# Moving left-over squares and late sums one place down ScalarE's list in the opening steps of a fused convolution and SoLU kernel

## The chip, the cores and the metric

The program runs on one core of a Trainium2 chip. The metric is the device time of one execution in microseconds (us), taken as the median of several runs. Each engine of the core (TensorE = PE, VectorE = DVE, ScalarE = ACT, GpSimd = POOL, SyncE = SP, which issues the transfers) works through a list of its own in order; semaphores tie the lists together.

## The reference

`x` is 8 x 4160 x 192. A causal convolution with 7 taps per head (softmax of `weight`) gives 33280 tokens of 192, and a SoLU layer follows:

```python
out = np.einsum('hk,bskhg->bshg', w, x_unf)        # convolution, 7 taps, 8 heads
h = x @ w_in                                       # 192 -> 1024
e = np.exp(h - h_max)
sm = e / (np.sum(e, axis=-1, keepdims=True) + 1e-09)
solu = h * sm
mu = np.mean(solu, axis=-1, keepdims=True)
var = np.mean((solu - mu) ** 2, axis=-1, keepdims=True)
ln = (solu - mu) / np.sqrt(var + 1e-06) * g_ln
return (ln @ w_out).astype(np.float32)             # 1024 -> 192
```

## The kernel before

The 33280 tokens are 260 tiles of 128 tokens. `x` is also cut into chunks: chunk 0 has 1024 rows (tiles 0 to 7), chunks 1 and 2 feed tiles 8 to 15 and 16 to 24 or so, and so on. A chunk is loaded, its size is measured (`sum_squares`: ACT squares or DVE maxima, "sums of x"), a scale is worked out by a short run of DVE instructions (`scale_steps`), and its convolution is done on PE in pieces (`product`, tiles `pc`). The result leaves PSUM as two fp16 parts: the upper by ACT (`upper`, line 313), the lower by DVE (`lower`, line 322), both into `y16`, which a transfer transposes into `yT`. From chunk 3 on the convolution takes `x` in two fp16 halves: `halve_steps` makes them in three steps for each piece of five windows: the upper half `xs` (ACT for chunk 3, line 234), the scaling of `x` (POOL, line 240) and the lower half (POOL, line 243). These steps lie in a `Queue` with a cost for each; `queue.run(budget)` puts as many of them into the lists as the budget allows.

A tile goes through these instructions: eight matmuls and a few small ones into `ph` (lines 736 and 759), `emit_max` (DVE, line 790), `emit_exp` (ACT, line 797), `emit_mul` (DVE, line 807), `emit_hi` (ACT cast to the fp16 half `p16`, line 815), `emit_lo` (POOL, the other half, line 827, and the transposing transfer `pT`, line 829), `emit_square` (ACT, line 819, a sum of squares for the variance), and some five tiles later `emit_out` (PE, `po`, line 859) and `emit_evac` (DVE, lines 867 and 869). `po`, `pc` and `tph` (a matmul that spreads the taps) take turns in two PSUM banks (`single`), so each of them waits until the one before the last has been read. `tph` is copied out by two small ACT casts (line 583).

From tile 8 on three tiles a, b, c form one call of `three_steps(i)`, for i = 8, 11, 14, 17, 20 and so on. The program is written by hand in the order of the lists: what is called earlier stands earlier on its engine. Calls with i < 16 (8, 11 and 14) have `start` set. What a call leaves over (the square of its last tile, in some calls also of tile b) is kept in `squares` and done in the next call by `root_squares()`. `late` holds sums of x that were put off. The last square of a group of eight tiles also puts the group's `steps` (POOL's inverse root) into the queue.

Of the kernel before, what the change touches and what calls it, by code (L numbers as in the profile page):

```python
# [19 lines left out]
def kernel(  # L20
# [533 lines left out]
    for e, bank in enumerate(banks):  # L554
        for q in range(2 * per):
# [4 lines left out]
                start=q == 0, stop=q == 2 * per - 1,  # L560
# [233 lines left out]
    def emit_exp(t):  # L794
        g, grp = t.g, t.grp
        t.e = sp.tile([P, F], F32, name=f"e_{t.i}", tag="e", bufs=4)
        act.activation(  # L797
            t.e, t.ph, AF.Exp, bias=t.bias, scale=-1.0, accum_out=grp.z[:, g : g + 1]
        )
# [12 lines left out]
    def emit_hi(t):  # L812
        t.halves = t.e.rearrange("p (n f) -> p n f", n=NH)
        t.p16 = sp.tile([P, NH, 2, 512], F16, name=f"p16_{t.i}", tag="p16", bufs=4)
        act.copy(t.p16[:, :, 0, :], t.halves)  # L815

    def emit_square(t):
        junk = sp.tile([P, F], F32, name=f"sq_{t.i}", tag="sq", bufs=1)
        act.activation(  # L819
            junk, t.e, AF.Square, accum_out=t.grp.s2[:, t.g : t.g + 1]  # L820
        )
        if t.g == t.grp.n - 1 and t.g:
            t.grp.squares()
            queue.put(t.grp.steps(), first=True)

    def emit_lo(t, eng):
        eng.tensor_tensor(t.p16[:, :, 1, :], t.halves, t.p16[:, :, 0, :], ALU.subtract)  # L827
        t.pT = sp.tile([P, 2 * NFC, P], F16, name=f"pT_{t.i}", tag="pT", bufs=4)
        nc.sync.dma_start_transpose(t.pT, t.p16.rearrange("p n a f -> p (n a f)"))
# [231 lines left out]
    queue, groups, chain, rooted, rows, stores = Queue(), {}, [], [], [], []  # L1061

    def follow(c, i):

        chain.extend(
            (c.add_up, i + 1 + (c.ch > 1)) if f is None else (f, None)
            for f in c.scale_steps()
        )

        def go():  # L1070
            c.scaled = True
            if c.exact:
                return
            for j in range(c.np):
                queue.put(c.halve_steps(j, quick=c.ch == 3), (c.ch, j))

        chain.append((go, None))
# [8 lines left out]
    def take_rooted():  # L1086
        for g, age in rooted:
            if age:
                g.ready = True
                rows.extend(g.waiting)  # L1090
        rooted[:] = [(g, 1) for g, age in rooted if not age]
# [25 lines left out]
    PAIRED = FIRST // P  # L1117
    assert spans[0][2] == PAIRED * P and PAIRED == 8 and (NT - PAIRED) % 3 == 0
    early, doubles, squares, late, moves = [], [], [], [], []
# [12 lines left out]
    def sum_up(c, h, i):  # L1132
        c.sum_squares(*h)
        if c.sums == 2 * c.np:
            c.square_peaks()
            follow(c, i)
# [158 lines left out]
    def three_steps(i):  # L1295
# [19 lines left out]

        start = i < 2 * PAIRED

        soon = i in (FIRST // P * 2 + 1, FIRST // P * 3 + 2)
        if not start:
            loads(work)  # L1320
# [16 lines left out]
        def second():  # L1337
            for d in done[1:2]:
                emit_out(d)
            place(2)  # L1340
# [4 lines left out]
        def uppers(n):  # L1345
            for k, pc, hg in at(n):
                if not k.scaled and k.exact:
                    run_chain(20)
                k.upper(pc, *hg)

        def lowers(n):
            for k, pc, hg in at(n):
                k.lower(pc, *hg)

        def move():

            for f in moves[:1]:
                f()
            del moves[:1]

        def root_squares():
            for q in squares:
                emit_square(q)
            squares.clear()

        def opens():
            for k in work.get("open", []):
                k.open(lefts[k.ch], chunks[k.ch - 1])

        def turns():  # L1370
            moves.extend(
                lambda k=k, q=q: k.turn(*q) for k, q in work.get("turn", [])
            )

        def openings():
            opens()
            turns()
            while moves:
                move()
# [13 lines left out]
        if start:  # L1393
            emit_max(a)
            emit_exp(a)
            if i == PAIRED:
                for k, h in late:
                    sum_up(k, h, i - 1)
        if not start:
            root_squares()  # L1400
        add(0)
        if not start:
# [6 lines left out]
        emit_max(b)  # L1409
        lowers(1)  # L1410
        emit_exp(b)
        if start:
            root_squares()
            second()
            if i > PAIRED:
                for k, h in late:
                    sum_up(k, h, i - 1)
                late.clear()
                uppers(2)
            for k, q in doubles:  # L1420
                k.double(*q)
            doubles.clear()
# [3 lines left out]
            late[:] = after  # L1426
        emit_hi(a)
        emit_lo(a, pool)
        move()
        if urgent:  # L1430
            openings()
# [55 lines left out]
            chunks[5].load(0)  # L1487
        emit_lo(c, pool)
        squares.append(c)
        if urgent:  # L1490
            for k, q in work["double"]:
                k.double(*q)
        elif start:
            openings()
            doubles.extend(work.get("double", []))
        else:
            opens()
            if not soon:
                turns()
            move()  # L1500
            doubles.extend(work.get("double", []))
        if i == NT - 6:
            ready(b)
        queue.run(3.8 if i < 20 else 2.0)
        take_rooted()

    def ready(t):
        emit_z(t)
        emit_root(t)
# [58 lines left out]
    for i in range(PAIRED, NT - 3, 3):  # L1568
        three_steps(i)
# [28 lines left out]
```

## Time and profile before

| what | value |
|---|---|
| runs | 1162.34, 1166.07, 1166.71 us (median 1166.07) |
| profiled execution, first to last instruction | 1161.5 us; its own whole time is not listed beside it |
| PE busy | 1132.2 us, 97% of the span |
| DVE, ACT, POOL busy | 1016.8, 998.0, 878.6 us |
| mean granted PE clock | 0.999 |

The span is 0.84 us under the fastest run and 4.6 us under the median. In the profile's rows a time is from the span's start; "idle before, releaser" is how long the engine stood still before the instruction and which instruction ended most of that.

### The profile page before, as it was taken

Reading aid. Unit: us, or ns where it says so; the run is one execution under the profiler, and the core shown is the slowest. Engines: PE = TensorE matmul, PEld = TensorE weight load, DVE = VectorE, ACT = ScalarE, POOL = GpSimd, SP = SyncE. Lnnn points to the kernel's source line nnn. Section 1 sums busy time; section 2 is a strip of 40 time slices with the busy share of each in tenths; the row PEclk is TensorE's granted clock in tenths of the full one; section 3 lists DMA queues with packets and bytes.
Section 4 is the critical chain, followed back from the end, with each engine's and each line's share of the span. In section 5 each row is a group of like instructions: output and inputs, shape, how many; then the busy total and the mean of one; then the engine's idle time right before and its main releaser. Section 6 shows DMA issues by size and latency. Waiting matters only on the chain.

```text
span 1161.5 us, 22374 instructions
## 1 busy us (share of the span) xinstructions
PE 1132.2 (97%) x7742; PEld 692.4 (60%) x7742; DVE 1016.8 (88%) x2058; ACT 998.0 (86%) x1775; POOL 878.6 (76%) x686
## 2 busy tenths in 40 slices
PE   5898999999999999999999999999999999999998
PEld 3575566656666665655656666665666566566556
DVE  8888898988989898998889989888898988788787
ACT  6998988888888888888888888898888889888886
POOL 2745879987888588887868888588788858855665
PEclk9999999999999999999999999999999999999999
DMA  8799899999999999999999999999999998999988
GB/s 226 171 181 180 185 218 205 205 201 202 200 213 195 195 186 220 207 189 199 202 198 190 208 209 199 187 202 208 206 204 198 195 193 170 174 177 186 181 163 188
DMA packets 727391, 226.95 MB, mean 195 GB/s; under 512 B 651614, under 2 KB 725870, under 8 KB 727278
## 3 DMA queue, kind: packets, MB, share of 16 engines
q1 hardware_dynamic: 727278, 225.53, 100.2%
q8 instruction: 60, 0.98, 0.3%
q14 instruction: 53, 0.43, 0.1%
HBM read 33.00 MB, written 25.56 MB: 50 GB/s over the span
## 4 chain that ended last, share of the span: by engine, by line
PE 88%; DVE 5%; ACT 2%; DMA 2%; issue 2%; POOL 1%; SPq 0%; DVEq 0%; ACTq 0%; POOLq 0%
PE po L859 40%; PE ph L736 36%; PE pc L281 6%; PE ph L759 5%; DVE e L807 1%; DMA pT<-p 1%; DVE ph L790 1%; DMA raw_in<-in_moe_w_in_dram 1%; ACT e L797 1%; ACT sq L819 0%; DVE raw L869 0%; DVE y L322 0%; POOL p L827 0%; PE mean L701 0%; DVE wlo L647 0%
## 5 line engine op out<-in xcount | busy, mean ns | idle before, releaser
L827 POOL TENSOR_TENSOR p<-e,p 128x1024 f16<-128x1024 f32 x257 | 548.3, 2138 | 219.5 <-ACT p L815 218.0
L859 PE MATMUL po<-ohl,pT 128*128 128x192 f16 (+1 forms) x4264 | 539.8, 283 | 7.8 <-DVE raw L869 5.4
L859 PEld LDWEIGHTS <-pT 128*128 128x128 f16 x4264 | 384.4, 98 | 167.1 <-issue 7.6
L736 PE MATMUL ph<-whi,yT 128*128 128x512 f16 x1548 | 419.1, 380 | 2.7 <-DVE e L807 2.6
L790 DVE TENSOR_SCALAR_CACHE_REDUCE ph<-ph,cv 128x1024 f32<-128x1024 f32 x248 | 319.1, 1288 | 72.9 <-PE ph L759 56.6
L797 ACT ACTIVATE e<-ph,sm 128x1024 f32<-128x1024 f32 x260 | 289.4, 1113 | 102.0 <-DVE ph L790 95.8
L807 DVE SCALAR_TENSOR_TENSOR e<-ph,cv,e 128x1024 f32<-128x1024 f32 x248 | 317.1, 1279 | 26.0 <-ACT e L797 25.7
L736 PEld LDWEIGHTS <-yT 128*128 128x128 f16 x2064 | 192.6, 98 | 231.3 <-issue 36.3
L815 ACT CAST p<-e 128x1024 f16<-128x1024 f32 x257 | 266.8, 1039 | 27.9 <-DVE e L807 27.3
L819 ACT ACTIVATE sq<-e 128x1024 f32<-128x1024 f32 x260 | 273.4, 1052 | 0.2
L736 PE MATMUL ph<-wlo,yT 128*128 128x512 f16 x516 | 153.5, 379 | 0.0
L869 DVE TENSOR_REDUCE raw<-po 128x192 f32<-128x384 f32 x247 | 136.3, 552 | 14.3 <-PE po L859 13.9
L243 POOL TENSOR_TENSOR xs<-xr,xs 128x960 f16<-128x960 f32 (+1 forms) x56 | 107.6, 1922 | 1.4
L313 ACT ACTIVATE y<-pc 112x432 f16<-112x432 f32 (+5 forms) x140 | 62.8, 469 | 13.8 <-PE pc L281 8.1
L759 PE MATMUL ph<-wlo,yT 64*128 64x512 f16 x269 | 74.0, 380 | 0.0
L322 DVE SCALAR_TENSOR_TENSOR y<-pc,y 112x432 f16<-112x432 f32 (+5 forms) x140 | 72.2, 532 | 0.8 <-ACT y L313 0.8
L281 PE MATMUL pc<-xs,taps_hi 128*112 128x240 f16 (+1 forms) x448 | 72.9, 261 | 0.0
L759 PE MATMUL ph<-wlo,y 64*128 64x512 f16 x251 | 68.6, 380 | 0.0
L181 DVE TENSOR_REDUCE xa<-xr 128x1 f32<-128x384 f32 x112 | 66.6, 617 | 0.0
L281 PEld LDWEIGHTS <-taps_hi 128*112 128x112 f16 x448 | 52.4, 130 | 16.4
L240 POOL TENSOR_SCALAR xr<-xr,s 128x960 f32<-128x960 f32 (+1 forms) x56 | 57.5, 1027 | 2.9
L281 PE MATMUL pc<-xs,taps_lo 128*112 128x240 f16 (+1 forms) x224 | 58.5, 261 | 0.0
(148 smaller groups left out, 787.6 us busy)
## 6 DMA issues: line engine op xcount, KB each, us to landing
out_dram<-raw SPq DMA_DIRECT2D x127, 192.0 KB, 3.0
xr<-in_x_dram SPq DMA_DIRECT2D x41, 480.0 KB, 4.7
xr<-in_x_dram SPq DMA_DIRECT2D x22, 384.0 KB, 4.1
pT<-p SPq DMA_TRANSPOSE x263, 4.6
y<-yT SPq DMA_DIRECT2D x15, 140.0 KB, 3.1
y<-yT SPq DMA_DIRECT2D x15, 126.0 KB, 3.1
yT<-y SPq DMA_TRANSPOSE x102, 3.7
raw_out<-in_moe_w_out_dram SPq DMA_DIRECT2D x1, 1536.0 KB
```

The source lines that it names most:

```text
L243: (2.1 * size + 0.2, lambda: pool.tensor_tensor(xl, r, h, ALU.subtract)),
L281: nc.tensor.matmul(o, tp[:, h + j, :], r, start=q == 0, stop=q == len(ops) - 1)
L736: nc.tensor.matmul(bank, lhs, w[:, r, n * 512 : (n + 1) * 512], start=start and j == 0, stop=stop and j == len(ops) - 1,)
L759: nc.tensor.matmul(banks_of(t)[n], y[q, t.off : t.off + P], wlo[q, 1, n * 512 : (n + 1) * 512], start=start, stop=not start,)
L790: dve.tensor_scalar(t.ph, t.ph, t.cv[:, 0:1], None, ALU.mult, ALU.min, accum_out=t.bias)
L797: act.activation(t.e, t.ph, AF.Exp, bias=t.bias, scale=-1.0, accum_out=grp.z[:, g : g + 1])
L807: dve.scalar_tensor_tensor(t.e, t.ph, t.cv[:, 3:4], t.e, ALU.mult, ALU.mult, accum_out=t.grp.s1[:, t.g : t.g + 1],)
L815: act.copy(t.p16[:, :, 0, :], t.halves)
L819: act.activation(junk, t.e, AF.Square, accum_out=t.grp.s2[:, t.g : t.g + 1])
L827: eng.tensor_tensor(t.p16[:, :, 1, :], t.halves, t.p16[:, :, 0, :], ALU.subtract)
L859: nc.tensor.matmul(t.po[:, 0:n], t.pT[:, a, :], w, start=j == 0, stop=j == len(ops) - 1)
L869: dve.tensor_reduce(t.grp.raw[:, t.g, :], t.po[:, 0 : 2 * D].rearrange("p (a d) -> p d a", a=2), AX.X, ALU.add,)
```

## The change

Four edits. In the calls with `start` (8, 11, 14) `root_squares()` and, for 11 and 14, the late sums go from right after the second exponential to behind the first cast (`emit_hi(a)`) and `emit_lo(a)`. In call 17 (`behind`) `root_squares()` goes from ahead of the first maximum to behind the second exponential. At the end of call 14 (`held`) the last `queue.run` is left out, so what it put into the lists comes with the next one, in the middle of call 17.

```diff
+        behind = i == 2 * PAIRED + 1
...
-        if not start:
+        if not start and not behind:
             root_squares()
...
         emit_exp(b)
+        if behind:
+            root_squares()
         if start:
-            root_squares()
             second()
             if i > PAIRED:
-                for k, h in late:
-                    sum_up(k, h, i - 1)
-                late.clear()
                 uppers(2)
...
         emit_hi(a)
         emit_lo(a, pool)
+        if start:
+            root_squares()
+            if i > PAIRED:
+                for k, h in late:
+                    sum_up(k, h, i - 1)
+                late.clear()
         move()
...
         squares.append(c)
+        held = i + 3 == 2 * PAIRED + 1
...
-        queue.run(3.8 if i < 20 else 2.0)
+        if not held:
+            queue.run(3.8 if i < 20 else 2.0)
```

The lists of PE, DVE and SP keep their order; those of ACT and POOL change. In the rows below the number behind a tile's name is that of the tile or chunk (`e_12` is tile 12, `xs_3` is chunk 3), the last number is only a counter.

ACT in call 8, before, from the second exponential on:

```order
L797 ACTIVATE e_9_761,z_8_690<-ph_9_729,sm_9_759 128x1024
L819 ACTIVATE sq_7_763,s2_0_270<-e_7_646 128x1024
L917 ACTIVATE t1_0_271<-z_0_268,cv_0_168 128x8
L921 ACTIVATE t2_0_272<-s1_0_269 128x8
L313 ACTIVATE y16_2_0_809<-pc_2_0_0_792,s_2_754 112x5x96
L815 CAST p16_8_811<-e_8_748 128x2x512
L819 ACTIVATE sq_8_825,s2_8_692<-e_8_748 128x1024
L815 CAST p16_9_828<-e_9_761 128x2x512
L313 ACTIVATE y16_2_0_809<-pc_2_0_4_841,s_2_754 112x5x32
```

and after:

```order
L797 ACTIVATE e_9_761,z_8_690<-ph_9_729,sm_9_759 128x1024
L313 ACTIVATE y16_2_0_805<-pc_2_0_0_788,s_2_754 112x5x96
L815 CAST p16_8_807<-e_8_748 128x2x512
L819 ACTIVATE sq_7_812,s2_0_270<-e_7_646 128x1024
L917 ACTIVATE t1_0_271<-z_0_268,cv_0_168 128x8
L921 ACTIVATE t2_0_272<-s1_0_269 128x8
L819 ACTIVATE sq_8_825,s2_8_692<-e_8_748 128x1024
L815 CAST p16_9_828<-e_9_761 128x2x512
L313 ACTIVATE y16_2_0_805<-pc_2_0_4_841,s_2_754 112x5x32
```

The square of tile 7 and its group's two small rows now stand behind the copy of the convolution and the cast of tile 8, so that copy is the next thing after the exponential. In calls 11 and 14 the same happens: in 11 two squares (tiles 9 and 10) and two sums of x change places with one copy (line 313) and the cast of tile 11; in 14 the squares of tiles 12 and 13 with two copies and the cast of tile 14.

POOL from the end of call 14 to call 20, before:

```order
L827 TENSOR_TENSOR p16_16_1232<-e_16_1215,p16_16_1232 128x2x512
L243 TENSOR_TENSOR xs_3_1227<-xr_3_0_329,xs_3_1227 128x960
L240 TENSOR_SCALAR xr_3_1_333<-xr_3_1_333,s_3_1054 128x960
L827 TENSOR_TENSOR p16_17_1311<-e_17_1304,p16_17_1311 128x2x512
L243 TENSOR_TENSOR xs_3_1227<-xr_3_1_333,xs_3_1227 128x960
L240 TENSOR_SCALAR xr_3_2_557<-xr_3_2_557,s_3_1054 128x960
L243 TENSOR_TENSOR xs_3_1227<-xr_3_2_557,xs_3_1227 128x960
L827 TENSOR_TENSOR p16_18_1348<-e_18_1308,p16_18_1348 128x2x512
```

and after:

```order
L827 TENSOR_TENSOR p16_16_1232<-e_16_1215,p16_16_1232 128x2x512
L827 TENSOR_TENSOR p16_17_1308<-e_17_1299,p16_17_1308 128x2x512
L243 TENSOR_TENSOR xs_3_1227<-xr_3_0_329,xs_3_1227 128x960
L240 TENSOR_SCALAR xr_3_1_333<-xr_3_1_333,s_3_1054 128x960
L827 TENSOR_TENSOR p16_18_1344<-e_18_1303,p16_18_1344 128x2x512
L243 TENSOR_TENSOR xs_3_1227<-xr_3_1_333,xs_3_1227 128x960
L240 TENSOR_SCALAR xr_3_2_557<-xr_3_2_557,s_3_1054 128x960
L243 TENSOR_TENSOR xs_3_1227<-xr_3_2_557,xs_3_1227 128x960
```

Each piece of chunk 3's lower half comes one `p16` later on POOL: the half of piece 1 (the row that reads `xr_3_1` into `xs_3`) now has the `p16` of tiles 17 and 18 ahead of it, where it had only that of tile 17. PE's first convolution of chunk 3, in call 20, reads pieces 0 and 1.

ACT in call 17, before, from the cast of tile 16 to that of tile 17:

```order
L815 CAST p16_16_1232<-e_16_1215 128x2x512
L234 ACTIVATE xs_3_1227<-xr_3_0_329,s_3_1054 128x960
L234 ACTIVATE xs_3_1227<-xr_3_1_333,s_3_1054 128x960
L583 CAST taps_hi_135<-tph_2_1276 128x2x8x14
L583 CAST taps_lo_136<-tph_2_1276 128x2x8x14
L936 ACTIVATE raw_0_550<-raw_0_550,t2_0_272 128x192
L819 ACTIVATE sq_16_1299,s2_16_1062<-e_16_1215 128x1024
L797 ACTIVATE e_17_1304,z_16_1060<-ph_17_1267,sm_17_1302 128x1024
L797 ACTIVATE e_18_1308,z_16_1060<-ph_18_1281,sm_18_1306 128x1024
L815 CAST p16_17_1311<-e_17_1304 128x2x512
```

and after:

```order
L815 CAST p16_16_1232<-e_16_1215 128x2x512
L234 ACTIVATE xs_3_1227<-xr_3_0_329,s_3_1054 128x960
L583 CAST taps_hi_135<-tph_2_1273 128x2x8x14
L583 CAST taps_lo_136<-tph_2_1273 128x2x8x14
L936 ACTIVATE raw_0_550<-raw_0_550,t2_0_272 128x192
L797 ACTIVATE e_17_1299,z_16_1060<-ph_17_1264,sm_17_1297 128x1024
L797 ACTIVATE e_18_1303,z_16_1060<-ph_18_1278,sm_18_1301 128x1024
L819 ACTIVATE sq_16_1305,s2_16_1062<-e_16_1215 128x1024
L815 CAST p16_17_1308<-e_17_1299 128x2x512
```

The upper half of piece 1 has gone behind the cast of tile 17 and the square of tile 16 behind both exponentials, so the two exponentials of call 17 have two long rows fewer ahead of them, and the cast of tile 17 one.

## The prediction

> **What bounds the kernel now.** First the page's share of each engine and the chain, then busy time by stretches, then PE's waits inside the stretch that the change touches.
>
> ```profile
> PE 1132.2 (97%) x7742; PEld 692.4 (60%) x7742; DVE 1016.8 (88%) x2058; ACT 998.0 (86%) x1775; POOL 878.6 (76%) x686
> ...
> PE 88%; DVE 5%; ACT 2%; DMA 2%; issue 2%; POOL 1%; SPq 0%; DVEq 0%; ACTq 0%; POOLq 0%
> ```
>
> ```profile
> 80.00:126.50 46.50, 41.11 (x284) 25.42 (x283) 36.25 (x78) 40.60 (x76) 28.77 (x25) 1.00 0.94 183
> 126.50:137.00 10.50, 10.30 (x74) 6.44 (x72) 10.28 (x21) 10.06 (x19) 10.42 (x6) 1.00 0.75 154
> 137.00:1155.00 1018.00, 1015.69 (x6937) 616.77 (x6937) 899.25 (x1806) 878.58 (x1554) 799.74 (x616) 1.00 1.03 197
> ```
>
> The columns are PE, its weight loads, DVE, ACT, POOL, the granted clock, DMA. From 137 us on PE stands still for 2.3 of 1018 us: whatever PE has lost or won by then arrives at the end almost one for one. Before, in the calls that are changed (8 to 17, about 65 to 126 us), PE is idle for 5.4 us, by this view of its waits from 80 to 140 us:
>
> ```profile
> PE po L859 <- DVE raw L869: 5.0, 5, 1.8
> PE pc L281 <- DVE y L322: 0.5, 1, 0.5
> PE tph L577 <- DVE y L322: 0.2, 1, 0.2
> ```
>
> So the prize is 5.7 us at most, 0.28 of it after the change's last place. PE waits for DVE to empty a PSUM bank, and DVE is late because it waits for ACT. ACT is 40.6 of 46.5 us busy; a new order moves its work, it takes none away.
>
> **The change, call by call.** Each number is a shift of the same row of before.
>
> *Call 8.* Rows of the timelines of DVE, ACT and PE:
>
> ```profile
> 71.53 0.15 DVE L112 TENSOR_SCALAR s<-s 128x1 int32<-128x1 int32 x1
> 70.67 1.05 ACT L819 ACTIVATE sq<-e 128x1024 f32<-128x1024 f32 x1
> 72.09 0.64 ACT L313 ACTIVATE y<-pc,s 112x480 f16<-112x480 f32 x1
> 75.67 0.81 ACT L313 ACTIVATE y<-pc,s 112x160 f16<-112x160 f32 x2
> 76.51 0.84 DVE L322 SCALAR_TENSOR_TENSOR y<-pc,s,y 112x160 f16<-112x160 f32 x2 [0.56 <-ACT y L313]
> 77.50 1.04 PE L281 MATMUL pc<-xr,taps 128*112 128x120 f32 x8
> ```
>
> The copy at 72.09 needs the scale `s`, ready at 71.68. Before, the square fills that time. Now the copy is next at 70.67 and ACT stands still until about 71.72: it wins 0.37 us for the copy and loses 1.05 for all that comes after the square. The copy at 75.67 starts 1.05 later, DVE's part at 76.51 with it (it was waiting for ACT by 0.56 already), and PE's convolution at 77.50 is released by it: it started 0.15 after DVE's end at 77.35. PE loses 1.05. Exponential, DVE product and cast follow each other from here without a gap in which 1.05 could be made up, and all carry it into call 11.
>
> *Call 11.*
>
> ```profile
> 83.96 1.05 ACT L819 ACTIVATE sq<-e 128x1024 f32<-128x1024 f32 x1
> 83.87 1.04 PE L281 MATMUL pc<-xr,taps 128*112 128x120 f32 x8
> 87.64 0.64 ACT L313 ACTIVATE y<-pc,s 112x480 f16<-112x480 f32 x1
> 88.32 0.72 DVE L322 SCALAR_TENSOR_TENSOR y<-pc,s,y 112x480 f16<-112x480 f32 x1 [2.86 <-ACT y L313]
> 91.97 2.12 PE L859 MATMUL po<-ohl,pT 128*128 128x384 f16 x16 [1.80 <-DVE raw L869]
> ```
>
> Here the move helps: two squares and two sums (83.96 to 87.64, 3.68 us) no longer stand ahead of the copy. It starts when PE's convolution is done, 83.87 + 1.05 + 1.0 = 85.9 instead of 87.64, with ACT idle for 0.9 us before it. DVE's part follows at 86.5. At the pace of the trace (88.32 to 91.97) the matmuls behind it could start at 90.2; PE itself, 1.05 late, is free for them at 90.5 instead of 91.97 and wins 1.5. The price is on ACT: 1.05 + 0.9 = 1.95 us later for everything behind the four moved rows.
>
> *Call 14.*
>
> ```profile
> 97.16 1.29 DVE L790 TENSOR_SCALAR_CACHE_REDUCE ph<-ph,cv 128x1024 f32<-128x1024 f32 x1 [0.33 <-PE ph L759]
> 101.92 1.05 ACT L819 ACTIVATE sq<-e 128x1024 f32<-128x1024 f32 x1
> 104.14 0.72 ACT L313 ACTIVATE y<-pc,s 112x128 f16<-112x128 f32 x2
> 104.89 0.17 DVE L203 TENSOR_REDUCE xm<-pc 128x1 f32<-128x8 f32 x1 [2.58 <-ACT y L313]
> 108.00 2.12 PE L859 MATMUL po<-ohl,pT 128*128 128x384 f16 x16 [1.30 <-DVE raw L869]
> 107.51 1.04 ACT L815 CAST p<-e 128x1024 f16<-128x1024 f32 x1 [0.66 <-DVE e L807]
> 109.30 1.11 ACT L797 ACTIVATE e<-ph,sm 128x1024 f32<-128x1024 f32 x1 [0.24 <-DVE s L112]
> ```
>
> DVE, fed by ACT's exponentials, comes to the first maximum (97.16) with 0.33 us of slack, so the maxima and exponentials here are 1.95 - 0.33, about 1.7 late. The two squares ahead of the copy (2.22 us) are gone, so the copy starts at 103.6 instead of 104.14, DVE's chain and the matmuls at 108.00 come 0.6 earlier. The squares now stand ahead of the cast of tile 15, which eats ACT's idle 0.66 + 0.24 us there; the exponential at 109.30 comes 0.6 later.
>
> *Call 17.*
>
> ```profile
> 113.11 2.08 ACT L234 ACTIVATE xs<-xr,s 128x960 f16<-128x960 f32 x2
> 116.95 1.10 ACT L797 ACTIVATE e<-ph,sm 128x1024 f32<-128x1024 f32 x1
> 119.51 1.04 ACT L815 CAST p<-e 128x1024 f16<-128x1024 f32 x1 [0.27 <-DVE e L807]
> 120.00 2.12 PE L859 MATMUL po<-ohl,pT 128*128 128x384 f16 x16 [1.19 <-DVE raw L869]
> 122.87 2.12 PE L859 MATMUL po<-ohl,pT 128*128 128x384 f16 x16 [0.46 <-DVE raw L869]
> 126.56 0.37 PE L281 MATMUL pc<-xs,taps_hi 128*112 128x240 f16 x2
> ```
>
> The exponential at 116.95 has one upper half (1.0) and one square (1.05) less ahead: 116.95 + 0.6 - 2.05 = 115.5. Both waits of PE go (DVE reads `po` in time), the matmuls of 122.87 start at 121.4, and PE is ready for the convolution of chunk 3 at 125.1, 1.5 before its time of 126.56. The cast of tile 17 comes at 119.51 + 0.6 - 1.0 - 0.27 = 118.85.
>
> *POOL, from call 14 to call 20.* This decides. Before:
>
> ```profile
> 115.97 2.13 POOL L827 TENSOR_TENSOR p<-e,p 128x1024 f16<-128x1024 f32 x1
> 118.06 2.00 POOL L243 TENSOR_TENSOR xs<-xr,xs 128x960 f16<-128x960 f32 x1
> 120.05 1.07 POOL L240 TENSOR_SCALAR xr<-xr,s 128x960 f32<-128x960 f32 x1
> 121.08 2.13 POOL L827 TENSOR_TENSOR p<-e,p 128x1024 f16<-128x1024 f32 x1
> 123.17 2.01 POOL L243 TENSOR_TENSOR xs<-xr,xs 128x960 f16<-128x960 f32 x1
> ```
>
> POOL ends piece 1's lower half at 125.17, 1.4 us before PE wants it (126.56). After, POOL waits after tile 16's `p16` (about 118) for the cast of tile 17, which ends at 119.8. From 119.85: `p16` of tile 17, 2.1; piece 0's lower half, 2.0; scaling, 1.05; `p16` of tile 18, 2.1; piece 1's lower half, 2.0; together 9.25, so 129.1. PE waits from 125.1 to 129.15, 4.0 us, and starts the convolution 2.6 later than before. All that is won is lost again and 2.6 more. DVE and ACT catch up in the wait, so the 0.28 us that PE waited at 137.08 goes: +2.3.
>
> Other queues: SP keeps its order. Some `pT` transfers start 1 to 2 us later, but PE reads tile 15's at 122.87, 15 us after its cast at 107.51. DVE's memset for chunk 5 waits until POOL has read piece 0 (124.0 now, 120.06 before), but DVE comes to it at about 126.5: free. POOL's `p16` of tiles 20 and 21 end 2 us later, less than PE's own shift.
>
> *The clock.* What a 4 us wait does to PE's clock, the opening stretch shows:
>
> ```profile
> 30.27 0.60 PE L736 MATMUL ph<-whi,yT 128*128 128x512 f16 x2 [1.69 <-DVE e L807]
> 34.48 2.98 PE L281 MATMUL pc<-xr,taps 128*112 128x120 f32 x16 [1.77 <-issue]
> ...
> 35.00:38.50 3.50, 3.50 (x19) 3.50 (x18) 2.63 (x9) 3.50 (x7) 3.50 (x3) 0.51 0.54 113
> ```
>
> Two gaps of 1.69 and 1.77 us within 6 us were followed by 3.5 us at half clock, 3.5 x 0.49 = 1.7 us of work lost. No other gap of before cost clock, not the 1.80 at 91.97 with 0.49 shortly before. One gap of 4.0 us has more idle time than both together, so I take the half clock: +1.7 (bounds 0 and 1.7; it can't hide, since PE then sets the pace).
>
> [...]
>
> **Sum.** On the profiled execution: +2.6 at the convolution of chunk 3, -0.28, +1.7: 1161.5 + 4.0 = 1165.5 us of span. The span lies 4.6 under the median of the runs, so on the median: 1166.07 + 4.0 = 1170.1. Bounds: cast of tile 17 as early as PE's and DVE's rows let it be, with nothing lost in call 8 (exponential at 113.6 after the maximum of tile 17, cast done at 118.0): lower half at 127.3, +0.7 - 0.28, and no clock lost: +0.4. The other end is +4.0 with another 2 us for what piles up behind.
>
> **The rivals.**
> 1. *The gain arrives.* Piece 1's lower half is ready when PE comes, by 121 to 125, and all of PE's waits go: 1166.07 - 5.7 = 1160.4; it decides at 126.56, the time of before: any earlier and the kernel wins. For it: 5.4 us of PE's idle time hang on the rows that are moved ahead. Against it: two `p16` of 2.1 each stand ahead of that half on POOL, and the second needs a cast that ACT reaches after everything it did before. 0.1.
> 2. *The wait without the clock.* Same sum without 1.7: 1168.4. For it: the gaps of before that left the clock alone. 0.25.
> 3. *A short wait.* ACT's loss in call 8 is made up, as in the lower bound: 1166.5 without clock, 1168.2 with it. For it: ACT is idle for 5.9 of the 46.5 us, though its idle rows wait for DVE's part of the same chain. 0.15.
> 4. *More piles up.* POOL's 2 us reach `pT` of later tiles: above 1172. Against it: the 15 us between a cast and its use on PE. 0.05.
>
> **How the numbers follow.** The forecast (wait of about 4 us, half clock, 1170.1) has 0.45, the rivals 0.1, 0.25, 0.15, 0.05. Runs of before spread over 4.4 us, so each case by 2 either way. The range 1163.5 to 1173 holds the forecast and rivals 2 and 3 and leaves out most of 1 and 4. Half a per cent, about what a measurement of this kernel can tell from none, is 5.8 us: under 1160.2 is faster, only half of rival 1, 0.05; above 1171.9 is slower, rival 4 and the upper fifth of the forecast, 0.15; the rest, 0.8, is the same.
>
> **What would show it.** In the profile after: a wait of some 4 us of PE's `pc` (line 281) at about 125 to 129, released by POOL's line 243; half clock just after; ACT idle for 1 us before the copy at 71.7; PE's convolution of 77.5 about 1 late; waits on DVE's line 869 down from 5.0 us to about 3. It is wrong if PE enters call 20's convolution before 126.5, or if what PE has lost by 140 us does not arrive at the end.

## The result, and the profile after

The changed kernel took 1167.29 us (median of 15 runs, 1164.92 to 1169.14), the kernel before 1163.88 us (median of 15, 1160.78 to 1166.71). The ratio is 1.0028, 95% interval 1.0019 to 1.0037: 3.4 us slower by the medians, within half a per cent. Here and below a ratio is estimated from all runs of a set, against the kernel before in that same set, so it need not be the quotient of the two medians. One execution below, of the queue's edit alone, took 6334 us; its ratio leaves it out and its trace isn't read. The profiled execution of the changed kernel took 1168.12 us for a span of 1166.1, so 2.0 us lie around the span; the span of before was 1161.5.

First PE's waits between 60 and 145 us of the changed kernel (us in total, times, longest), to be read against the three rows of before:

```profile
PE pc L281 <- POOL xs L243: 3.7, 1, 3.7
PE pc L281 <- DVE y L322: 2.7, 3, 1.3
PE po L859 <- DVE raw L869: 0.8, 2, 0.4
PE ph L759 <- DVE e L807: 0.4, 1, 0.4
```

The waits for DVE to empty `po` have nearly gone (5.0 to 0.8 us). The waits for the lower part of the first convolutions have grown (0.5 to 2.7), and one wait is new and longer than any other: 3.7 us for POOL's line 243. POOL's own timeline says where it comes from:

```profile
115.89 2.14 POOL L827 TENSOR_TENSOR p<-e,p 128x1024 f16<-128x1024 f32 x1
119.18 2.13 POOL L827 TENSOR_TENSOR p<-e,p 128x1024 f16<-128x1024 f32 x1 [1.15 <-ACT p L815]
121.27 2.02 POOL L243 TENSOR_TENSOR xs<-xr,xs 128x960 f16<-128x960 f32 x1
123.26 1.07 POOL L240 TENSOR_SCALAR xr<-xr,s 128x960 f32<-128x960 f32 x1
124.30 2.14 POOL L827 TENSOR_TENSOR p<-e,p 128x1024 f16<-128x1024 f32 x1
126.39 2.01 POOL L243 TENSOR_TENSOR xs<-xr,xs 128x960 f16<-128x960 f32 x1
```

and PE's timeline shows the one matmul on piece 0 that still gets ahead, and the wait behind it:

```profile
124.44 0.27 PE L281 MATMUL pc<-xs,taps_hi 128*112 128x240 f16 x1
128.45 0.36 PE L281 MATMUL pc<-xs,taps_hi 128*112 128x240 f16 x1 [3.74 <-POOL xs L243]
```

The last POOL row is piece 1's lower half. It ends at 128.40 and PE starts at 128.45. The `p16` of tiles 17 and 18 (119.18 and 124.30) stand ahead of it, and POOL stood idle for 1.15 us until ACT had cast tile 17.

What followed on PE's clock, in windows (span, PE, its weight loads, DVE, ACT, POOL, granted clock, DMA share, GB/s):

```profile
126.90:133.70 6.80, 5.25 (x18) 2.07 (x18) 2.05 (x4) 4.65 (x8) 6.72 (x5) 0.50 1.17 179
133.70:137.00 3.30, 3.30 (x26) 2.35 (x25) 2.79 (x5) 1.35 (x3) 2.45 (x2) 1.00 1.06 211
140.00:1155.00 1015.00, 1012.39 (x6890) 612.83 (x6889) 896.12 (x1794) 874.43 (x1546) 799.12 (x615) 1.00 1.02 195
```

The granted clock was 0.50 from 126.9 to 133.7 and PE worked in it for 5.25 us; half of that, 2.6, is lost by an estimate from these two numbers. After 140 us PE again has no slack (idle for 2.6 us of 1015).

Executions start a little earlier or later, so I compare them from one PE row, the matmul that adds up the size of chunk 2, to the same for chunk 4. Of before, then of after:

```profile
70.43 0.29 PE L95 MATMUL pc<-xa,ones 128*128 128x8 f32 x2
...
141.38 0.29 PE L95 MATMUL pc<-xa,ones 128*128 128x8 f32 x2
```

```profile
69.73 0.29 PE L95 MATMUL pc<-xa,ones 128*128 128x8 f32 x2
...
145.38 0.29 PE L95 MATMUL pc<-xa,ones 128*128 128x8 f32 x2
```

That stretch, called the marker below, takes 70.95 us before and 75.65 after, 4.7 more. From the later row to the end of the span before takes 1020.1 and after 1020.7 us. So nearly all of the difference between these two executions arises between 70 and 145 us.

### The profile page after: what moved, and what is told of

Read it like the earlier page. It is cut to its first block, busy times and chain, and to the rows that moved or that the text cites. A ratio compares the mean times of both kernels' runs of the same rounds, so it can differ in the third digit from the quotient of the medians.

```text
span 1166.1 us, 22374 instructions
## 1 busy us (share of the span) xinstructions
PE 1135.1 (97%) x7742; PEld 693.1 (59%) x7742; DVE 1016.2 (87%) x2058; ACT 997.8 (86%) x1775; POOL 879.5 (75%) x686
## 4 chain that ended last, share of the span: by engine, by line
PE 87%; DVE 6%; ACT 3%; issue 2%; DMA 1%; POOL 1%; POOLq 0%; SPq 0%; DVEq 0%; ACTq 0%
PE po L859 39%; PE ph L736 36%; PE pc L281 6%; PE ph L759 5%; DVE e L807 1%; DVE ph L790 1%; DMA pT<-p 1%; ACT sq L819 1%; DVE y L322 1%; ACT p L815 1%; ACT e L797 0%; ACT y L313 0%; POOL xs L243 0%; POOL p L827 0%; PE mean L701 0%
## 5 line engine op out<-in xcount | busy, mean ns | idle before, releaser
L240 POOL TENSOR_SCALAR xr<-xr,s 128x960 f32<-128x960 f32 (+1 forms) x56 | 57.7, 1031 | 2.9
L281 PE MATMUL pc<-xs,taps_lo 128*112 128x240 f16 (+1 forms) x224 | 58.7, 262 | 0.0
```

Source lines behind the costliest of these rows:

```text
L281: nc.tensor.matmul(o, tp[:, h + j, :], r, start=q == 0, stop=q == len(ops) - 1)
```

## The experiments

The theory: the loss comes from the `queue.run` left out at the end of call 14, through POOL and then the clock. The rivals: ACT's 1 us in call 8, the clock alone, or the moved squares.

**The queue as before** (the change without its `held`; nothing else differs):

```diff
-        if not held:
-            queue.run(3.8 if i < 20 else 2.0)
+        queue.run(3.8 if i < 20 else 2.0)
```

> The changed kernel with its fourth edit undone: the last queue run of call 14 is done again, so piece 1's lower half of chunk 3 has only one p16 ahead of it on POOL, as before; the squares and sums stay moved. Theory POOL (the loss is piece 1's lower half coming behind two p16, and the half clock after that wait): POOL ends the half at about 125.2, PE comes for it at about 125.3, no wait of PE's line 281 on POOL's line 243 above 0.5 us, clock full, and the time is about 0.8 us below before (ratio 0.999). Rival ACT (the moved squares themselves cost, by ACT's idle time in call 8): it stays 2 to 3 us above before (ratio 1.002 to 1.003).

1163.50 against 1162.84 us, ratio 1.0005 [0.9996, 1.0013]; the loss is gone. PE's waits between 60 and 145 us:

```profile
PE pc L281 <- DVE y L322: 2.7, 3, 1.3
PE po L859 <- DVE raw L869: 2.3, 4, 0.8
PE ph L759 <- DVE e L807: 0.4, 1, 0.4
```

No wait on POOL. But no gain either, where 0.999 was expected: PE's waits are 5.4 us in sum, where before had 5.7, and the marker takes 71.17 us, 0.2 more than before. What the moved rows win in `po` is paid back on line 322, 1.28 us of it at the convolution of call 8.

**The queue alone** (the kernel before with only this; run in two sets, and the rows are from the second):

```diff
-        queue.run(3.8 if i < 20 else 2.0)
+        if i + 3 != 2 * PAIRED + 1:
+            queue.run(3.8 if i < 20 else 2.0)
```

> The kernel before with the fourth edit alone: the last queue run of call 14 left out, squares and sums where they were. Theory POOL: two p16 stand ahead of piece 1's lower half, it ends near 128.5 instead of 125.17, PE waits about 3 us for it, and the time is 1.8 us (clock full) to 3.5 us (half clock) above before, ratio 1.0015 to 1.003. Rival ACT: no loss, ratio 0.999 to 1.000.

> The same kernel as the one with the fourth edit alone, once more for its profile, since the execution that was profiled there took 6332 us and shows nothing. Theory POOL: PE waits 3 us or more for POOL's line 243 in its first convolution of chunk 3, half clock behind it, ratio 1.003 to 1.004 as measured there. Rival: the loss shows at another row.

1.0041 [1.0027, 1.0055] and 1.0023 [1.0010, 1.0036]: on both sides of the whole change's 1.0028. The second one's profile has the wait without any square moved; its waits between 60 and 145 us, PE's row, and the clock:

```profile
PE po L859 <- DVE raw L869: 3.8, 4, 1.8
PE pc L281 <- POOL xs L243: 3.1, 1, 3.1
PE pc L281 <- DVE y L322: 0.4, 1, 0.4
```

```profile
126.68 0.26 PE L281 MATMUL pc<-xs,taps_hi 128*112 128x240 f16 x1 [3.08 <-POOL xs L243]
```

```profile
125.00:130.00 5.00, 3.32 (x21) 1.60 (x21) 2.19 (x5) 4.20 (x7) 4.92 (x4) 1.00 1.26 187
130.00:135.00 5.00, 5.00 (x38) 3.34 (x37) 5.00 (x9) 4.15 (x9) 4.92 (x4) 1.00 0.96 214
```

In this execution the granted clock stayed at 1.00 after a wait of 3.08 us, against what was expected, and it is one of the two fastest of its set (1163.02 us). The marker is 2.1 above before. Of the twelve runs of this set, the four with a mean granted clock of 0.996 or less average 1168.1 us, the other eight 1165.1.

**Call 8 as before** (the change, with this line added ahead of `second()` for call 8 alone, and the later call to it finding nothing left):

```diff
         if start:
+            if i == PAIRED:
+                root_squares()
             second()
```

> The changed kernel with call 8 alone as before. Theory POOL: ACT comes to the cast of tile 17 about 1 us earlier, so piece 1's lower half ends about 1 us earlier; PE still waits 3.5 us or so for it and its clock still falls, and the time is about 1 us below the changed kernel, ratio 1.002. Rival ACT (call 8's idle time is the whole loss): ratio 1.000.

1167.86 against 1163.36 us, 1.0037 [1.0024, 1.0050], where 1.002 was expected: no faster than the whole change, so the loss is not call 8's. Everything up to the wait is earlier by what call 8 had lost, POOL's half too, and the wait stays:

```profile
129.42 0.36 PE L281 MATMUL pc<-xs,taps_hi 128*112 128x240 f16 x1 [3.73 <-POOL xs L243]
```

From the first marker row (71.70 here) this is 57.7 us, 1.0 less than in the changed kernel (128.45 - 69.73 = 58.7). The marker takes only 0.65 less than in the changed kernel. PE works at half clock for longer here: the granted clock is 0.50 in all of 130 to 135 us, and since the 16 `po` matmuls from 135.29 on take 2.16 us, where they take 2.12 elsewhere, I estimate that PE works in it until 135.35, for 5.9 us from 129.42, against 5.25.

```profile
130.00:135.00 5.00, 5.00 (x17) 1.62 (x16) 1.86 (x3) 2.81 (x5) 4.92 (x4) 0.50 1.25 168
```

**Call 8 and the queue as before** (both of the edits above):

> The changed kernel with two things undone: the last queue run of call 14 is done again, and in call 8 the left-over square stands right behind the second exponential as before. What stays of the change: the squares (and sums) moved in calls 11, 14 and 17. Theory POOL plus call 8 (the moved square leaves ACT idle for 1 us in call 8, which PE then waits for): PE's wait of 1.3 us for its convolution in call 8 goes, no wait on POOL's line 243, and the total of chunk 4's sums on PE, 71.2 us behind that of chunk 2 with the queue run alone put back, comes at about 70.2 us; the time is about 0.8 us below before, ratio 0.999. Rival (call 8 is hidden behind later waits): as with the queue run alone put back, ratio 1.0005.

1162.55 against 1163.36 us, 0.9999 [0.9989, 1.0009]. The waits on line 322 fall from 2.7 to 1.4, the marker takes 70.19 us, 0.8 less than before and 1.0 less than with the queue alone put back. So call 8 costs 1 us of the marker, and what is left of the moved rows, in calls 11, 14 and 17, is worth 0.8 us in the profile, too little for the runs to tell.

**Piece 1 ahead of one `p16`** (the change, with a larger budget in the middle of call 17):

```diff
-        queue.run(3.8 if i < 20 else 2.0)
+        queue.run(5.8 if behind else 3.8 if i < 20 else 2.0)
```

> The changed kernel with a larger budget (5.8 in place of 3.8) for the queue run in the middle of call 17: on POOL piece 1's lower half changes places with the p16 of tile 18, nothing else moves. Theory POOL: the half ends at about 126.3 instead of 128.4, PE's wait falls from 3.7 to about 1.7 us, the clock stays full, and the time is within 0.5 us of before (ratio 1.000). Rival ACT: as the changed kernel, ratio 1.003.

1164.65 against 1162.84 us, 1.0009 [1.0000, 1.0018]. POOL now does piece 1's half ahead of tile 18's `p16`:

```profile
123.45 2.01 POOL L243 TENSOR_TENSOR xs<-xr,xs 128x960 f16<-128x960 f32 x1
125.42 2.13 POOL L827 TENSOR_TENSOR p<-e,p 128x1024 f16<-128x1024 f32 x1
```

```profile
125.51 0.26 PE L281 MATMUL pc<-xs,taps_hi 128*112 128x240 f16 x1 [1.76 <-POOL xs L243]
```

The wait is 2.0 us shorter, one `p16`, and in this execution the granted clock is 1.00 from 102 to 142 us. By the ratios two thirds of the loss are gone, by the medians half, with nothing else moved. The eleven runs fall in two groups, five from 1162.1 to 1162.7 us and six from 1164.6 to 1166.2; the profiled one is the fastest of all, and what parts the groups is not shown.

**The clock kept up by other work** (the change, with 16 matmuls of 512 columns, written into a bank that is overwritten anyway, ahead of chunk 3's first convolution; and once more with 8 columns, as a stand-in for the issue of the same matmuls without their work):

```diff
+            if self.ch == 3 and a == 0 and h == 0:
+                for _ in range(16):
+                    nc.tensor.matmul(
+                        bank, whi[:, 0, 0:P], whi[:, 0, 0:512], start=True, stop=True
+                    )
```

> The changed kernel with 16 matmuls of 512 columns more in front of the first convolution of chunk 3, into the same PSUM bank, whose result is overwritten; they take some 3.5 us and lie in PE's wait of 3.7 us. Theory POOL with the clock: the wait for POOL's line 243 is as long, but the clock stays full from 125 to 135 us, and the time is 1 to 2.6 us below the changed kernel: 1 to 2 us above before, ratio 1.001. If the clock does not matter (PE's half speed hidden behind other work): the same as the changed kernel, ratio 1.003.

> The same kernel as the one with 16 added matmuls in PE's wait, once more, since its five runs (1165.2 to 1169.2 us) can't tell 1.002 from 1.004. The profile of that one had the full clock and chunk 4's total 2.2 us later than before, counted from chunk 2's total. Theory (half clock costs time): ratio 1.002, under the changed kernel's 1.0028. Rival (it does not, or other waits take its place): ratio 1.003 or more.

> Control for the two runs with 16 added matmuls, which kept the clock full but were no faster than the changed kernel (ratios 1.0037 and 1.0043 against 1.0028): the same 16 matmuls in the same place, of 8 columns in place of 512, so PE has as many instructions but stands idle for most of the wait. Theory (half clock costs some 2.5 us, and the added instructions cost about as much elsewhere): the clock falls again and the time is 2 us above those two, ratio 1.006. Rival (half clock costs nothing in the end): ratio 1.004, as those two. Second rival (the added matmuls' length, not their number, cost the 2 us): ratio 1.003, as the changed kernel.

The added lines push the convolution to line 286. The three: 1.0037 [1.0023, 1.0051], 1.0043 [1.0029, 1.0056], and 1.0046 [1.0030, 1.0061] with the tiny ones. PE's row after the wide ones, and after the tiny ones, then the windows of the tiny ones:

```profile
127.98 0.26 PE L286 MATMUL pc<-xs,taps_hi 128*112 128x240 f16 x1 [0.28 <-POOL xs L243]
```

```profile
127.63 0.26 PE L286 MATMUL pc<-xs,taps_hi 128*112 128x240 f16 x1 [3.30 <-POOL xs L243]
```

```profile
125.00:130.00 5.00, 2.37 (x13) 0.97 (x13) 2.14 (x5) 4.53 (x7) 4.92 (x4) 0.85 1.24 182
130.00:135.00 5.00, 5.00 (x31) 2.92 (x30) 3.42 (x8) 2.19 (x3) 4.92 (x4) 0.81 0.91 202
```

In the stretch itself the theory holds. The convolution starts 58.7 us after the first marker row in the changed kernel and in all three of these. With the wide matmuls the marker is then 2.2 above before (both times), 2.5 less than with the changed kernel, about the 2.6 estimated for its half clock (the granted clock is 1.00 from 125 to 135 us in the first wide run); with the tiny ones it is 3.9 above, with the granted clock at 0.85 and 0.81 in the two windows shown. The total times don't follow: none is lower than the changed kernel's 1.0028. In the traces most of what is missing stands at the end of the kernel, ahead of PE's last outputs (the changed kernel, then the first wide run, then the tiny ones):

```profile
1161.37 1.16 PE L859 MATMUL po<-ohl,pT 128*128 128x192 f16 x12 [0.20 <-DMA pT<-p]
1159.21 2.26 PE L864 MATMUL po<-ohl,pT 128*128 128x192 f16 x24 [1.84 <-DMA pT<-p]
1160.20 2.25 PE L864 MATMUL po<-ohl,pT 128*128 128x192 f16 x24 [2.13 <-DMA pT<-p]
```

The second wide run waits 1.92 us at the same place. Since the tiny ones wait as well, this goes with the added instructions and not with their length; how they bring it about is not shown. The three sets have five or six runs each and their intervals overlap, so they don't settle what the clock costs in the median.

**The half ahead of both `p16`** (the change with call 8 as before, and both budgets set so that piece 0's half comes ahead of tile 17's `p16` and piece 1's ahead of tile 18's; run in two sets):

```diff
-        queue.run(3.8 if i < 20 else 2.0)
+        queue.run(4.0 if behind else 3.8 if i < 20 else 2.0)
...
-        if not held:
-            queue.run(3.8 if i < 20 else 2.0)
+        queue.run(2.0 if held else 3.8 if i < 20 else 2.0)
```

> A version made to win: the changed kernel with call 8 as before, with a budget of 2.0 for the last queue run of call 14 (it places the lower half of piece 0 alone) and 4.0 for the one in the middle of call 17 (scaling and lower half of piece 1). On POOL piece 1's lower half has only the p16 of tile 17 ahead of it, as before, and on ACT its upper half no longer stands ahead of the exponentials of call 17. Theory POOL: PE waits about 0.8 us or less for line 243, clock full, chunk 4's total comes about 69.2 us after chunk 2's (before 70.95; with call 8 and the queue put back 70.2), and the time is 1.7 us below before, ratio 0.9985. Rival: what is won in calls 8 to 20 is lost again in later waits for the pT transfers, ratio 1.000.

> The version made to win once more, since its interval [0.9979, 1.0000] touches 1. Theory POOL: ratio 0.999 again, under 1 over both runs together. Rival: no difference, 1.000.

1161.65 against 1163.05 us, 0.9990 [0.9979, 1.0000], and 1162.17 against 1163.43 us, 0.9988 [0.9979, 0.9997]: ahead of the kernel before by a tenth of a per cent, the lowest ratio of all versions. The first one's waits between 60 and 145 us, and its POOL:

```profile
PE po L859 <- DVE raw L869: 1.8, 4, 0.7
PE pc L281 <- DVE y L322: 1.4, 2, 0.9
PE pc L281 <- POOL xs L243: 0.6, 1, 0.6
```

```profile
118.02 2.13 POOL L827 TENSOR_TENSOR p<-e,p 128x1024 f16<-128x1024 f32 x1
120.13 1.07 POOL L240 TENSOR_SCALAR xr<-xr,s 128x960 f32<-128x960 f32 x1
121.28 2.01 POOL L243 TENSOR_TENSOR xs<-xr,xs 128x960 f16<-128x960 f32 x1
```

PE gets to chunk 3 at 123.35 us, 54.6 after the first marker row, where before needs 56.1. The marker takes 70.18 us (69.2 was expected), only 0.8 less than before: 1.0 of the 1.6 us is lost again in two waits on line 869, where before lost 0.28. That is the marker of the version with call 8 and the queue as before (70.19), so the profile shows no gain of the new budgets over that one, and the runs can't tell the two apart either. The two waits:

```profile
131.22 2.12 PE L859 MATMUL po<-ohl,pT 128*128 128x384 f16 x16 [0.32 <-DVE raw L869]
134.66 2.12 PE L859 MATMUL po<-ohl,pT 128*128 128x384 f16 x16 [0.70 <-DVE raw L869]
```

**Call 17 and the budgets alone** (the kernel before, with `behind` and the two budgets just shown, but the squares and sums of calls 8, 11 and 14 where they were):

> The kernel before with only call 17's part of that version: the left-over square behind the second exponential and the two queue budgets (2.0 and 4.0); the squares of calls 8, 11 and 14 stay where they were. PE's waits of 1.8 and 1.3 us on DVE's line 869 in calls 11 and 14 are then there again. If what is won there reaches the end, chunk 4's total comes 0.5 to 1 us later after chunk 2's than the 70.2 us of the version made to win, and the ratio is 0.9995 to 1.000. Rival (ACT and POOL set the pace in calls 17 and 20, and what PE wins in calls 11 and 14 it waits for there): 70.2 us again, ratio 0.999.

1163.18 against 1163.43 us, 0.9993 [0.9983, 1.0003]: not to be told from before, nor from the version just shown, so the share of calls 11 and 14 in the total stays open. Its profiled execution answers another question. The prediction quoted PE's row at 91.97 us of before, 2.12 us long after a wait of 1.80. The same place here, and the window around it:

```profile
88.24 1.07 PE L281 MATMUL pc<-xr,taps 128*112 128x120 f32 x8 [0.49 <-DVE y L322]
91.11 3.71 PE L859 MATMUL po<-ohl,pT 128*128 128x384 f16 x16 [1.80 <-DVE raw L869]
```

```profile
91.00:95.00 4.00, 3.89 (x18) 2.37 (x18) 3.60 (x8) 2.32 (x4) 2.56 (x3) 0.57 1.00 144
```

The same gap of 1.80, 1.1 us after one of 0.49, was followed by a granted clock of 0.57 from 91 to 95 us here and by 1.00 over the same window there. It cost 3.71 - 2.12 = 1.6 us, and the marker of this execution is 1.5 above before. Without these 1.6 it would be 70.8 us by this estimate, 0.7 above the version just shown, as expected if calls 11 and 14 win something.

## Why the prediction was right or wrong

**The place and the cause: right.** The first sign named, a wait of some 4 us of `pc` on POOL's line 243, is there. The changed execution runs 0.70 us ahead of before at the first marker row; with that added, piece 1's half ends at 129.1 (said: 129.1), the first convolution on it starts at 129.15 (129.15), the cast of tile 17 at 118.75 (118.85), by this row of ACT:

```profile
118.05 1.06 ACT L815 CAST p<-e 128x1024 f16<-128x1024 f32 x1
```

Its loss against 126.56 is the predicted 2.6. The queue's edit alone gives a loss of the same size, with the same wait on POOL's row, its undoing takes all of it away, and one `p16` moved out of the way shortens the wait by just one `p16`. This shows that the loss starts with POOL's order.

**Call 8: right.** ACT stood still for 0.99 us ahead of the copy and PE waited 1.28 for the lower part:

```profile
71.06 0.66 ACT L313 ACTIVATE y<-pc,s 112x480 f16<-112x480 f32 x1 [0.99 <-issue]
```

```profile
77.79 1.04 PE L281 MATMUL pc<-xr,taps 128*112 128x120 f32 x8 [1.28 <-DVE y L322]
```

With the queue as before this is worth 1.0 us in the marker, where 1.05 was forecast. In the changed kernel undoing it takes 0.65 off the marker, and the runs don't show it (1.0037 against 1.0028).

**Waits on line 869: wrong in size.** I said 5.0 would fall to about 3; it fell to 0.8. What I had left there turned up elsewhere: of the 2.7 us on line 322 only 1.28 is call 8's, forecast above, and the other 1.4 (0.94 and 0.50, where before had 0.5) and 0.4 on line 807 are waits that I had not seen. The sum ahead of chunk 3 was still right, since it was made from the shifts and not from these waits.

**The clock: right in kind, mis-sized.** The term was +1.7, from 3.5 us at half clock. In the profiled execution the half clock lasted 6.8 us and cost 2.6 by the estimate above. So that execution lost 2.6 - 0.28 + 2.6 = 4.9 by my steps, against 4.7 in the marker and 4.6 in the span, where I had 4.0. Over the runs it is smaller: the eight of the fifteen with a mean granted clock of 0.996 or less average 1167.95 us, the other seven (0.997 and 0.998) 1165.91. A median of +3.4 lies between the sum with the clock and the one without (rival 2, +2.3). How many executions had the half clock at this place these mean clocks don't tell, since other spells enter them too: the traces of before and of the tiny matmuls both give 0.999, before with its one spell at 35 us (0.50 for 3.41 us), the tiny matmuls with one here (0.85 and 0.81 in the two windows above).

**The base: the largest part of the miss.** Of the 2.8 us between 1170.1 and 1167.29, 2.2 are the base: 1166.07 was the median of three runs, fifteen give 1163.88. The step that failed is "the span lies 4.6 under the median of the runs, so on the median". In the changed kernel's profile 2.0 us lie around the span; 1161.5 + 2.0 would have said 1163.5 for that execution, well under the median of three, and the forecast would have been 1167.5.

**The rivals.** The gain (1) did not come: PE was ready for chunk 3 1.4 us sooner, and POOL was later still. The wait without the clock (2) is not what the profiled execution shows; for the executions without a trace it stays open. The short wait (3) falls, since tile 17's cast came where the forecast had it and not at 118.0. The pile-up (4) falls too: from chunk 4's total to the end the changed execution loses only another 0.6 us against before.

## What to carry to other kernels

When work is moved down one engine's list to let something else go first, follow also what the moved code feeds on other engines: here an ACT list was reordered and the time was decided by one queue call that pushed a POOL step behind two `p16` instead of one. The wait of PE, which sets the pace, cost twice, once as a gap of 3.74 us and again in a granted clock of 0.50 after it (2.6 us by the estimate above), so the step that ends the longest gap should not stand behind work that is wanted later (here, a `p16`): with call 8 left as it was, moving it ahead turned a loss of 0.4% into a gain of 0.1%, and leaving the queue call where it had been did as well within what the runs can tell. And before adding a predicted difference to a median of few runs, compare that median with the profiled execution's own time.

## What the runs showed of the hardware

In the changed kernel the granted clock was 0.50 from 34.69 to 38.10 us and from 126.85 to 133.68, for 3.41 and 6.83 us, and 1.00 in the rest of 16 to 1155 us. In before it was 0.50 from 35.05 to 38.46, for 3.41 us. After the tiny matmuls and at the `po` wait above the windows (0.85 and 0.81 of 5 us each, 0.57 of 4 us) give 3.4 us of half clock, by an estimate from them. In these spells of 3.4 us PE worked throughout; in the one of 6.83 us it still stood in its wait until 128.45.

Whether a gap brings a spell was not set by its length alone: 3.74 us (the changed kernel), 3.73 (call 8 as before) and 3.30 (the tiny matmuls) did, 3.08 (the queue alone) and 1.76 (piece 1 ahead of one `p16`) did not, 1.80 did in one execution and not in another of a program that is the same up to there. The idle time of PE in the 3.4 us before does not settle it either. Windows (span, then PE) of the changed kernel, ahead of both of its falls, and of the last experiment, ahead of its fall:

```profile
31.28:34.69 3.41, 1.65 (x12) 1.06 (x12) 3.14 (x7) 3.41 (x6) 3.33 (x2) 1.00 0.54 103
123.43:126.85 3.42, 1.28 (x7) 0.59 (x6) 2.65 (x7) 3.42 (x7) 3.42 (x3) 1.00 1.07 205
88.03:91.44 3.41, 1.40 (x11) 1.17 (x12) 3.26 (x7) 3.41 (x7) 2.70 (x4) 1.00 0.17 38
```

and of before, at the same place of the program as the third, where the granted clock stayed at 1.00:

```profile
88.89:92.30 3.41, 1.41 (x11) 1.18 (x12) 3.26 (x7) 3.41 (x7) 2.70 (x4) 1.00 0.01 2
```

PE is idle for 1.8, 2.1 and 2.0 us in the first three and for 2.0 in the last. What decides is not shown.
